# Linear attention on one core: the order of the last three heads, the engines that divide them, and the PSUM banks of the last numerators

## The chip, the cores and the metric

The kernel runs on one core of a Trainium2 chip. The metric is device time in microseconds for one execution. Three executions of the kernel before took 171.89 to 172.21 us, with a median of 172.04 us.

## The reference

Inputs q, k and v are bf16, each of shape (1, 32, 2048, 128): 32 heads, 2048 rows, 128 columns. For every head:

```
phi_q = where(q > 0, q + 1, exp(q)) + 1e-6
phi_k = where(k > 0, k + 1, exp(k)) + 1e-6
kv  = phi_k^T v          # 128 x 128
z   = sum of phi_k over the rows
num = phi_q kv           # 2048 x 128
den = phi_q z + 1e-6     # 2048
out = num / den
```

The kernel uses where(x > 0, x + 1, exp(x)) = min(exp(x), 1) + max(x, 0), and feeds the two summands to TensorE one after the other, so that PSUM adds them.

## The kernel before

**Tiles.** A head's 2048 rows lie as 128 partitions of 16 tiles ("tile" t, 0 to 15, each 128 columns wide). One head is 512 KB in each of k, v and q, and 512 KB of output. There are 6 input buffers per tensor (NBI) and 10 output buffers (NBO).

**Work of one head.**
- SP loads k, v and q (L255), one DMA each.
- ScalarE (ACT in the profile) takes exp of k (L263) and GpSimd (POOL) its positive part (L265). VectorE (DVE) makes min(exp, 1) + 1e-6 (L269, "emk"). For five of the 16 tiles, GpSimd adds the two parts (L274, the tag "phik").
- TensorE (PE) accumulates kv and z in one PSUM bank, kvz_ps (L285, L288). I call the block kv(h).
- ScalarE copies kv to kvs_sb (L294, "kvs"); VectorE adds z as its first column (L296, "zs").
- PE transposes q in two halves of 8 tiles into the two banks of xT_ps (L304). ScalarE takes exp of both halves (L315) and the positive part of the second half (L318, "relu"). VectorE takes the positive part of the first half (L321, "rq") and finishes emq (L324).
- PE multiplies phi_q with kvs (L333, L334) into the five banks of o_ps: three tiles to a bank, tile 15 split over banks 0 and 1. I call the block num(h).
- VectorE adds 1e-6 to the denominators (L352, "den"), inverts them (L356), and multiplies: tile 15 (L364), then tiles 0 to 5 and 6 to 14 (L369). For heads 30 and 31 the denominators are treated in two groups (banks 0 and 1, then 2 to 4), tiles 6 to 11 go to VectorE, and tiles 12 to 14 to ScalarE (L378, three instructions).
- SP stores the head (L394): one DMA, and three for head 31 (tiles 0 to 5, 6 to 11, 12 to 15).

**What sets the order.** Each piece of work is given to a small planner with an engine and a key (a number near the head's index). Each engine runs its pieces by rising key. The planner finds the dependences from named tags and puts in the semaphore waits. Two rules matter below: a piece that writes a bank waits for all readers of it on other engines, and two engines that read one bank take turns (L39). The list `place` (L239 to L242) sets keys by hand. The default keys of head h that matter are: on PE, kv h-1.2, transposes h-1.25, num h+0.7; on ScalarE, exp of q h-1.1, relu h-1.0, kvs h-0.95; on VectorE, zs h-0.095, rq h-1.052, emq h-1.045, den h+0.9. A store's key is h + 1.0 + 0.18 h, which puts the stores of the last heads behind all loads in SP's queue. The store waits for all the tiles that it holds, and SP issues in order. At the end SP waits for every output semaphore (L121).

In `place`, head 31 has its kv on PE at key 30.75, behind num(30), and its kvs and zs keys agree with that.

Of the kernel before, what the change touches and what calls it, by code (L numbers as in the profile page):

```python
# [4 lines left out]
ACT = mybir.ActivationFunctionType  # L5
ALU = mybir.AluOpType
P = 128
EPS = 1e-6
# [3 lines left out]
def _ap(base: bass.AP, elem_offset: int, dims):  # L12
    return bass.AP(base.tensor, base.offset + elem_offset, [list(base.ap[0])] + [list(d) for d in dims])
# [131 lines left out]
def bass_standalone__linear_attn_elu__prompt_kernel(  # L145
# [6 lines left out]
    B, H, S, D = q.shape  # L152
    assert D == P and S == 16 * P
    NT = 16
    NH = B * H
    bf16 = mybir.dt.bfloat16
    fp32 = mybir.dt.float32
    NBI = 6
    NBO = 10
    NC = D + 1  # L160
    NB = 5
# [4 lines left out]
    GAP, GRP = 32, 8 * D  # L166
    VW = 2 * GRP + 3 * GAP

    qf = q.rearrange("b h s d -> (b h) s d")
    kf = k.rearrange("b h s d -> (b h) s d")  # L170
    vf = v.rearrange("b h s d -> (b h) s d")
# [2 lines left out]
    with ExitStack() as es:  # L174
        def sb(name, shape, dt):
            return es.enter_context(nc.sbuf_tensor(name, shape, dt))
# [12 lines left out]
        rden_sb = sb("rden_sb", [P, 3, 4 * NB], fp32)  # L189
        o_sb = sb("o_sb", [P, NBO, NT, D], bf16)  # L190
        ident = sb("ident", [P, P], bf16)
        ones_sb = sb("ones_sb", [P, 1], bf16)

        xT_ps = es.enter_context(nc.psum_tensor("xT_ps", [P, NT * P], bf16))
        kvz_ps = es.enter_context(nc.psum_tensor("kvz_ps", [P, 512], fp32))
        o_ps = es.enter_context(nc.psum_tensor("o_ps", [P, NB * 512], fp32))

# [3 lines left out]
        def dma_sem(name):  # L201
            return dsems[name]

        for n, c in (("k", NBI), ("q", NBI), ("v", NBI), ("o", NBO + 2)):
            for i in range(c):
                dsems[(n, i)] = es.enter_context(nc.semaphore(f"s_{n}{i}"))

        block = es.enter_context(nc.Block())
        pl = Plan()

        def rows(x, h):
            return x[h].rearrange("(p j) d -> p (j d)", j=NT)

        ofull = o_ps[:, :]

        pl.add("pool", -9, lambda g: g.memset(ident[:], 0.0), writes=[("id0",)])
        pl.add("pool", -8, lambda g: g.affine_select(out=ident[:], in_=ident[:], compare_op=ALU.not_equal, fill=1.0,
# [1 line left out]
               reads=[("id0",)], writes=[("ident",)])  # L219
# [5 lines left out]
        def warm(n):  # L225

            def f(pe):
                for w in range(n):
# [10 lines left out]
        place = {("emk", 0): -2.05, ("rq", 0): -2.0, ("emq", 0): -1.9, ("zs", 0): -1.75,  # L239
                 ("emk", 1): -1.8, ("rq", 1): -1.7, ("emq", 1): -1.6, ("emk", 2): -1.4, ("rq", 2): 0.945,  # L240
                 ("ek", 1): -0.97, ("ek", 2): 0.03,
                 ("kv", NH - 1): NH - 2 + 0.75, ("kvs", NH - 1): NH - 2 + 0.05, ("zs", NH - 1): NH - 2 + 0.942}  # L242

        for h in range(NH):
            def at(name, key, h=h):
# [2 lines left out]
            bi, b2, b3, bo = h % NBI, h % 2, h % 3, h % NBO  # L248

            def load(name, buf, src, key, h=h, bi=bi):  # L250
                dst, rws = buf[:, bi], rows(src, h)
                if name == "v":
# [24 lines left out]

            def kv(pe, tiles, srcs, bi=bi, b3=b3):
                for j in tiles:
# [12 lines left out]
                   reads=[("emk", b3), ("rk", b3), ("v", bi), ("ones",), ("vones",)], writes=[("bankkv",)])  # L292
            pl.add("pe", at("kv", -1.2), lambda pe, kv=kv: kv(pe, ADD, (rk_sb,)), reads=[("phik", b3), ("v", bi)], writes=[("bankkv",)])
            pl.add("act", at("kvs", -0.95), lambda a, b3=b3: a.activation(kvs_sb[:, b3, 1:], kvz_ps[:, 1:NC], ACT.Copy),  # L294
                   reads=[("bankkv",)], writes=[("kvs", b3)])
            pl.add("dve", at("zs", -1 + 0.905), lambda d, b3=b3: d.tensor_scalar(  # L296
                kvs_sb[:, b3, 0:1], kvz_ps[:, 0:1], kvz_ps[:, NC:NC + 1], None, op0=ALU.add),
                   reads=[("bankkv",)], writes=[("zs", b3)])
# [14 lines left out]
            for half in (0, 1):  # L313
                pl.add("act", h - 1.1 + 0.05 * half,
                       lambda a, b2=b2, c=cols(half): a.activation(eq_sb[:, b2, c], xT_ps[:, c], ACT.Exp),  # L315
                       reads=[("bankx", half)], writes=[("eq", b2, half)])
            pl.add("act", h - 1.0,
                   lambda a, b3=b3, c=cols(1): a.activation(rq_sb[:, b3, c], xT_ps[:, c], ACT.Relu),  # L318
                   reads=[("bankx", 1)], writes=[("rq", b3, 1)])
            pl.add("dve", at("rq", -2 + 0.948),  # L320
                   lambda d, b3=b3, c=cols(0): d.tensor_scalar(rq_sb[:, b3, c], xT_ps[:, c], 0.0, None, op0=ALU.max),  # L321
                   reads=[("bankx", 0)], writes=[("rq", b3, 0)])
            pl.add("dve", at("emq", -2 + 0.955),
                   lambda d, b2=b2, b3=b3: d.tensor_scalar(emq_sb[:, b3, :], eq_sb[:, b2, :], 1.0, EPS, op0=ALU.min, op1=ALU.add),  # L324
                   reads=[("eq", b2, 0), ("eq", b2, 1)], writes=[("emq", b3)])


            phi = [("emq", b3), ("rq", b3, 0), ("rq", b3, 1), ("kvs", b3), ("zs", b3)]

            def num(bank, b3=b3):  # L330
                def tile(pe, t, col, c0, c1):
                    o_ap = o_ps[:, bank * 512 + col: bank * 512 + col + c1 - c0]
                    pe.matmul(o_ap, lhsT=emq_sb[:, b3, t * P:(t + 1) * P], rhs=kvs_sb[:, b3, c0:c1], start=True, stop=False)  # L333
                    return pe.matmul(o_ap, lhsT=rq_sb[:, b3, t * P:(t + 1) * P], rhs=kvs_sb[:, b3, c0:c1],  # L334
                                     start=False, stop=True)

                def f(pe):
                    for s in range(3):
                        last = tile(pe, bank * 3 + s, s * NC, 0, NC)
                    if bank < 2:  # L340
                        last = tile(pe, NT - 1, 3 * NC, 64 * bank, 64 * bank + 65)
                    return last
                return f
            for bank in range(NB):
                pl.add("pe", h + 0.7 + 0.001 * bank, num(bank), reads=phi, writes=[("banko", bank)])


            tail = h >= NH - 2
            for g, (b0, b1) in enumerate(((0, 2), (2, NB)) if tail else ((0, NB),)):
                key = h + 0.9 + 0.03 * g  # L350
                banks = [("banko", b) for b in range(b0, b1)]
                pl.add("dve", key, lambda d, b3=b3, b0=b0, b1=b1: d.tensor_scalar(  # L352
                    den_sb[:, b3, 4 * b0:4 * b1].rearrange("p (a b) -> p a b", b=4),
                    _ap(ofull, 512 * b0, [[512, b1 - b0], [NC, 4]]), EPS, None, op0=ALU.add),
                    reads=banks, writes=[("den", b3, g)])
                pl.add("dve", key + 0.01, lambda d, b3=b3, b0=b0, b1=b1: d.reciprocal(  # L356
                    rden_sb[:, b3, 4 * b0:4 * b1], den_sb[:, b3, 4 * b0:4 * b1]),
                    reads=[("den", b3, g)], writes=[("rden", b3, g)])

            def rd(col, dims, b3=b3):  # L360
                return _ap(rden_sb[:, b3, col:col + 1], 0, dims)

            def last_tile(d, bo=bo, rd=rd):
                return d.tensor_tensor(  # L364
                    out=o_sb[:, bo, NT - 1, :].rearrange("p (a b) -> p a b", b=64),
                    in0=_ap(ofull, 3 * NC + 1, [[512, 2], [1, 64]]), in1=rd(3, [[0, 2], [0, 64]]), op=ALU.mult)

            def div(b0, b1, bo=bo, rd=rd):
                return lambda d: d.tensor_tensor(  # L369
                    out=o_sb[:, bo, 3 * b0:3 * b1, :].rearrange("p (a b) d -> p a b d", b=3),  # L370
                    in0=_ap(ofull, 512 * b0 + 1, [[512, b1 - b0], [NC, 3], [1, D]]),
                    in1=rd(4 * b0, [[4, b1 - b0], [1, 3], [0, D]]), op=ALU.mult)

            def div_act(bank, bo=bo, rd=rd):
                def f(a):
                    for s in range(3):
                        c = 512 * bank + NC * s + 1
                        last = a.activation(o_sb[:, bo, 3 * bank + s, :], o_ps[:, c:c + D], ACT.Copy,  # L378
                                            scale=rd(4 * bank + s, [[1, 1]]))
                    return last  # L380
                return f

            lo, hi = ("rden", b3, 0), ("rden", b3, 1 if tail else 0)
            pl.add("dve", h + 0.92, last_tile, reads=[("banko", 0), ("banko", 1), lo], writes=[("o", bo, "t")])
            pl.add("dve", h + 0.925, div(0, 2), reads=[("banko", 0), ("banko", 1), lo], writes=[("o", bo, 0)])
            if tail:
                pl.add("dve", h + 0.945, div(2, 4), reads=[("banko", 2), ("banko", 3), hi], writes=[("o", bo, 1)])
                pl.add("act", h + 0.95, div_act(4), reads=[("banko", 4), hi], writes=[("o", bo, 2)])
            else:
                pl.add("dve", h + 0.945, div(2, NB), reads=[("banko", b) for b in (2, 3, 4)] + [hi],  # L390
                       writes=[("o", bo, 1), ("o", bo, 2)])

            def store(t0, t1, key, parts, slot, h=h, bo=bo):
                pl.add("sp", key, lambda sp: sp.dma_start(rows(of, h)[:, t0 * D:t1 * D],  # L394
                                                          o_sb[:, bo, t0:t1].rearrange("p j d -> p (j d)")),
                       reads=[("o", bo, p) for p in parts], dma=("o", slot))

            late = h + 1.0 + 0.18 * h
            if h < NH - 1:
                store(0, NT, late, ("t", 0, 1, 2), bo)  # L400
            else:
                store(0, 6, late, (0,), bo)
                store(6, 12, late + 0.01, (1,), NBO)
                store(12, 16, late + 0.02, ("t", 2), NBO + 1)

        pl.emit(block, sems, dma_sem)

# [27 lines left out]
```

## Time and profile before

| | |
|---|---|
| median of three executions | 172.04 us (171.89 to 172.21) |
| the profiled execution's own time | 171.87 us |
| its span, first to last instruction | 170.1 us |
| what lies around the span | 1.77 us |
| busy: PE, DVE, ACT, POOL | 158.0, 150.9, 155.0, 105.6 us |
| moved by DMA | 67.56 MB, mean 397 GB/s |
| mean granted TensorE clock | 0.99 |
| last VectorE multiplication ends | 166.43 us |
| last DMA lands | 169.6 us |

Times below are microseconds from the start of the span. "Landing" is the time from the issue of a DMA until the last of its 16 completion signals. The mean DMA share is that of 16 DMA engines, so 0.62 is about ten engines busy. In a list of instructions, a bracket shows how long the engine was idle just before and what released it.

### The profile page before, as it was taken

How to read it: one execution, taken by the hardware profiler on the slowest of the kernel's cores; microseconds unless marked ns; L12 is line 12 of the kernel's file. 1: busy time of each engine (PE TensorE's matmuls, PEld its weight loads, DVE VectorE, ACT ScalarE, POOL GpSimd, SP SyncE). 2: the span in 40 equal slices, each digit the busy share in tenths (PEclk: the TensorE clock that was granted, in tenths of full speed). 3: DMA queues.
4: the chain of work that ended last, by engine and by line, in shares of the span. 5: the costliest groups of instructions: out<-in, count | busy, mean ns of one | idle time of the engine just before them, and what ended most of it. 6: DMA issues, size and time to landing. Idle time of an engine off the chain costs nothing.

```text
span 170.1 us, 7091 instructions
## 1 busy us (share of the span) xinstructions
PE 158.0 (93%) x3108; PEld 155.8 (92%) x3108; DVE 150.9 (89%) x292; ACT 155.0 (91%) x167; POOL 105.6 (62%) x72
## 2 busy tenths in 40 slices
PE   6779999999999999999999999999999999997950
PEld 6669999999999999999999999999989999997940
DVE  0344999999999999999999999999998999999971
ACT  3899999999999999999999999999999999996331
POOL 3766777766666677766666667776666567655000
PEclk9999999999999999999999999999999999999996
DMA  5999999999999999999999999999999999999975
GB/s 220 333 415 408 418 408 406 415 412 408 411 411 412 411 417 411 412 414 410 412 416 410 413 414 410 409 416 413 411 416 412 413 412 411 412 415 413 410 302 196
DMA packets 22846, 67.56 MB, mean 397 GB/s; under 512 B 2080, under 2 KB 2464, under 8 KB 22816
## 3 DMA queue, kind: packets, MB, share of 16 engines
q1 hardware_dynamic: 22816, 67.12, 99.1%
q8 instruction: 24, 0.39, 0.9%
q14 instruction: 6, 0.05, 0.1%
HBM read 50.33 MB, written 16.78 MB: 395 GB/s over the span
## 4 chain that ended last, share of the span: by engine, by line
PE 68%; DVE 18%; DMA 6%; SPq 3%; issue 1%; ACT 0%; DVEq 0%
PE kvz_ps L285 29%; PE o_ps L333 13%; PE o_ps L334 13%; PE xT_ps L304 12%; DVE o_sb L369 8%; DMA v_sb<-in_v_dram 6%; SPq L255 3%; DVE rq_sb L321 2%; DVE emq_sb L324 2%; DVE emk_sb L269 2%; DVE o_sb L364 1%; DVE rden_sb L356 1%; PE kvz_ps L288 1%; DVE den_sb L352 1%; DVE kvs_sb L296 1%
## 5 line engine op out<-in xcount | busy, mean ns | idle before, releaser
L274 POOL TENSOR_TENSOR rk_sb<-rk_sb,emk_sb 128x640 bf16<-128x640 bf16 x32 | 44.7, 1398 | 46.9 <-DVE emq_sb L324 42.8
L369 DVE TENSOR_TENSOR o_sb<-o_ps,rden_sb 128x768 bf16<-128x768 f32 x64 | 70.1, 1134 | 0.0
L315 ACT ACTIVATE eq_sb<-xT_ps 128x1024 bf16<-128x1024 bf16 x64 | 66.7, 1170 | 3.1 <-PE xT_ps L304 3.0
L263 ACT ACTIVATE ek_sb<-k_sb 128x2048 bf16<-128x2048 bf16 x32 | 66.6, 2080 | 2.0 <-DMA k_sb<-in_k_dram 1.9
L285 PE MATMUL kvz_ps<-v_sb,rk_sb 128*128 128x128 bf16 (+1 forms) x512 | 67.0, 218 | 0.0
L333 PE MATMUL o_ps<-kvs_sb,emq_sb 128*128 128x129 bf16 (+1 forms) x544 | 62.0, 217 | 1.9 <-DVE o_sb L369 1.2
L265 POOL TENSOR_SCALAR rk_sb<-k_sb 128x2048 bf16<-128x2048 bf16 x32 | 60.7, 1896 | 3.8 <-DMA k_sb<-in_k_dram 3.0
L334 PE MATMUL o_ps<-kvs_sb,rq_sb 128*128 128x129 bf16 (+1 forms) x544 | 62.0, 217 | 0.0
L285 PE MATMUL kvz_ps<-v_sb,emk_sb 128*128 128x128 bf16 (+1 forms) x352 | 54.7, 218 | 2.6 <-DMA v_sb<-in_v_dram 1.1
L333 PEld LDWEIGHTS o_ps<-kvs_sb,emq_sb 128*128 128x128 bf16 x544 | 51.3, 98 | 2.3 <-DVE o_sb L369 1.5
L288 PE MATMUL kvz_ps<-ones_sb,rk_sb 128*128 128x1 bf16 x384 | 52.6, 165 | 0.0
L334 PEld LDWEIGHTS o_ps<-kvs_sb,rq_sb 128*128 128x128 bf16 x544 | 50.9, 97 | 0.0
L285 PEld LDWEIGHTS kvz_ps<-v_sb,rk_sb 128*128 128x128 bf16 x512 | 46.8, 97 | 0.0
L318 ACT ACTIVATE rq_sb<-xT_ps 128x1024 bf16<-128x1024 bf16 x32 | 37.8, 1180 | 0.0
L288 PE MATMUL kvz_ps<-ones_sb,emk_sb 128*128 128x1 bf16 x224 | 36.9, 166 | 0.0
L285 PEld LDWEIGHTS kvz_ps<-v_sb,emk_sb 128*128 128x128 bf16 x352 | 33.5, 97 | 3.6 <-DMA v_sb<-in_v_dram 2.4
L288 PEld LDWEIGHTS kvz_ps<-ones_sb,rk_sb 128*128 128x128 bf16 x384 | 35.0, 96 | 0.0
L304 PE MATMUL xT_ps<-ident,q_sb 128*128 128x128 bf16 x512 | 34.2, 220 | 0.5 <-DMA q_sb<-in_q_dram 0.4
L304 PEld LDWEIGHTS xT_ps<-ident,q_sb 128*128 128x128 bf16 x512 | 30.1, 98 | 1.1 <-DMA q_sb<-in_q_dram 0.9
L269 DVE TENSOR_SCALAR emk_sb<-ek_sb 128x2048 bf16<-128x2048 bf16 x32 | 21.8, 682 | 9.8 <-ACT ek_sb L263 9.8
L321 DVE TENSOR_SCALAR rq_sb<-xT_ps 128x1024 bf16<-128x1024 bf16 x32 | 21.7, 679 | 1.3 <-ACT eq_sb L315 1.3
L324 DVE TENSOR_SCALAR emq_sb<-eq_sb 128x2048 bf16<-128x2048 bf16 x32 | 22.0, 687 | 0.4 <-ACT eq_sb L315 0.4
(18 smaller groups left out, 79.2 us busy)
## 6 DMA issues: line engine op xcount, KB each, us to landing
k_sb<-in_k_dram SPq DMA_DIRECT2D x32, 512.0 KB, 13.6
q_sb<-in_q_dram SPq DMA_DIRECT2D x32, 512.0 KB, 13.1
v_sb<-in_v_dram SPq DMA_DIRECT2D x32, 512.0 KB, 13.4
out_dram<-o_sb SPq DMA_DIRECT2D x31, 512.0 KB, 13.7
out_dram<-o_sb SPq DMA_DIRECT2D x2, 192.0 KB, 3.2
out_dram<-o_sb SPq DMA_DIRECT2D x1, 128.0 KB, 2.8
```

The source lines that it names most:

```text
L263: lambda a, bi=bi, b2=b2: a.activation(ek_sb[:, b2, :], k_sb[:, bi, :], ACT.Exp),
L265: pl.add("pool", h, lambda g, bi=bi, b3=b3: g.tensor_scalar(rk_sb[:, b3, :], k_sb[:, bi, :], BIG, 0.0, op0=ALU.min, op1=ALU.max), reads=[( ...
L274: pl.add("pool", h + 0.5, lambda g, added=added: g.tensor_tensor(out=added(rk_sb), in0=added(rk_sb), in1=added(emk_sb), op=ALU.add), reads ...
L285: last = pe.matmul(kvz_ps[:, 1 - l:NC + r], lhsT=w, rhs=v_sb[:, bi, c - l:c + D + r], start=first, stop=fin, skip_group_check=True)
L288: last = pe.matmul(kvz_ps[:, 0:1], lhsT=w, rhs=ones_sb[:, 0:1], start=False, stop=fin, skip_group_check=True)
L304: last = pe.transpose(xT_ps[:, j * P:(j + 1) * P], q_sb[:, bi, j * P:(j + 1) * P], ident[:])
L315: lambda a, b2=b2, c=cols(half): a.activation(eq_sb[:, b2, c], xT_ps[:, c], ACT.Exp),
L318: lambda a, b3=b3, c=cols(1): a.activation(rq_sb[:, b3, c], xT_ps[:, c], ACT.Relu),
L324: lambda d, b2=b2, b3=b3: d.tensor_scalar(emq_sb[:, b3, :], eq_sb[:, b2, :], 1.0, EPS, op0=ALU.min, op1=ALU.add),
L333: pe.matmul(o_ap, lhsT=emq_sb[:, b3, t * P:(t + 1) * P], rhs=kvs_sb[:, b3, c0:c1], start=True, stop=False)
L334: return pe.matmul(o_ap, lhsT=rq_sb[:, b3, t * P:(t + 1) * P], rhs=kvs_sb[:, b3, c0:c1], start=False, stop=True)
L369: return lambda d: d.tensor_tensor(out=o_sb[:, bo, 3 * b0:3 * b1, :].rearrange("p (a b) d -> p a b d", b=3), in0=_ap(ofull, 512 * b0 + 1, ...
```

## The change

Only the pieces of heads 29, 30 and 31 change; the code for the others is rewritten so that it makes the same instructions in the same order.

- The two banks of transposed q become a float32 tensor x_ps of the same size, read as bf16 for the transposes. The numerators of head 31 for tiles 0 to 5 and 15 (banks 0 and 1) are written to it, not to o_ps.
- Head 29: VectorE divides tiles 0 to 5, 6 to 8 and 15; ScalarE divides tiles 9 to 14.
- Heads 30 and 31: VectorE divides tiles 0 to 2, 6 to 11 and 15; ScalarE divides tiles 3 to 5 and 12 to 14.
- kv(31) goes back to its default key 29.8 on PE, in front of num(30). On VectorE, rq(31) and emq(31) get keys in front of their default ones but behind the divisions of head 29; zs(31) stands right behind the first reciprocal of head 30. On ScalarE, kvs(31) stands behind the divisions of head 29 and in front of relu(31).
- Head 30 is stored in two DMAs (tiles 0 to 5, 6 to 15). Head 31 keeps three. One more output semaphore is there for this.

```diff
+    REST = ((0, NB, 0.9, (("dve", 0, 6), ("dve", 6, 15))),)
+    TAIL = {
+        NH - 3: ((0, NB, 0.9, (("dve", 0, 6), ("dve", 6, 9), ("act", 9, 15, 0.96))),),
+        NH - 2: ((0, 2, 0.9, (("dve", 0, 3), ("act", 3, 6, 0.96))),
+                 (2, NB, 0.93, (("dve", 6, 12), ("act", 12, 15, 0.97)))),
+        NH - 1: ((0, 2, 0.9, (("dve", 0, 3), ("act", 3, 6, 0.96))),
+                 (2, NB, 0.93, (("dve", 6, 12), ("act", 12, 15, 0.97)))),
+    }
+    PIECES = {NH - 2: ((0, 6), (6, NT)), NH - 1: ((0, 6), (6, 12), (12, NT))}
+    EXTRA = {NH - 2: 0, NH - 1: 1}
...
-        xT_ps = es.enter_context(nc.psum_tensor("xT_ps", [P, NT * P], bf16))
+        x_ps = es.enter_context(nc.psum_tensor("x_ps", [P, 1024], fp32))
...
-                 ("kv", NH - 1): NH - 2 + 0.75, ("kvs", NH - 1): NH - 2 + 0.05, ("zs", NH - 1): NH - 2 + 0.942}
+                 ("rq", NH - 1): NH - 3 + 0.925, ("emq", NH - 1): NH - 3 + 0.93, ("zs", NH - 1): NH - 2 + 0.9105,
+                 ("kvs", NH - 1): NH - 2 - 0.03}
...
+            def nbank(b, h=h):
+                return ("bankx", b) if h == NH - 1 and b < 2 else ("banko", b)
...
-                pl.add("pe", h + 0.7 + 0.001 * bank, num(bank), reads=phi, writes=[("banko", bank)])
+                pl.add("pe", h + 0.7 + 0.001 * bank, num(bank), reads=phi, writes=[nbank(bank)])
...
+            def div_act(t0, t1, bo=bo, rd=rd, nfull=nfull):
+                def f(a):
+                    for t in range(t0, t1):
+                        b, c = t // 3, 512 * (t // 3) + NC * (t % 3) + 1
+                        last = a.activation(o_sb[:, bo, t, :], _ap(nfull(b), c, [[1, D]]), ACT.Copy,
+                                            scale=rd(4 * b + t % 3, [[1, 1]]))
+                    return last
+                return f
...
+                for n, (eng, t0, t1, *place_a) in enumerate(runs):
+                    pl.add(eng, h + place_a[0] if eng == "act" else key + 0.012 + 0.004 * n,
+                           div_act(t0, t1) if eng == "act" else div(t0, t1),
+                           reads=[nbank(b) for b in range(t0 // 3, (t1 + 2) // 3)] + [("rden", b3, g)],
+                           writes=[("o", bo, t) for t in range(t0, t1)])
...
-            if h < NH - 1:
-                store(0, NT, late, ("t", 0, 1, 2), bo)
-            else:
-                store(0, 6, late, (0,), bo)
-                store(6, 12, late + 0.01, (1,), NBO)
-                store(12, 16, late + 0.02, ("t", 2), NBO + 1)
+            for n, (t0, t1) in enumerate(PIECES.get(h, ((0, NT),))):
+                store(t0, t1, late + 0.01 * n, bo if n == 0 else NBO + EXTRA[h] + n - 1)
```

More of the change, by code (lines that the diff above doesn't have):

```diff
@@ L202, in dma_sem @@
             return dsems[name]
-        for n, c in (("k", NBI), ("q", NBI), ("v", NBI), ("o", NBO + 2)):
+        for n, c in (("k", NBI), ("q", NBI), ("v", NBI), ("o", NBO + 3)):
             for i in range(c):
@@ L212, in rows @@
             return x[h].rearrange("(p j) d -> p (j d)", j=NT)
-        ofull = o_ps[:, :]
+        ofull, xfull = o_ps[:, :], x_ps[:, :]
+        xT_ps = xfull.bitcast(bf16)
         pl.add("pool", -9, lambda g: g.memset(ident[:], 0.0), writes=[("id0",)])
@@ L328, in bass_standalone__linear_attn_elu__prompt_kernel, with nfull, num @@
             phi = [("emq", b3), ("rq", b3, 0), ("rq", b3, 1), ("kvs", b3), ("zs", b3)]
-            def num(bank, b3=b3):
+            def nbank(b, h=h):
+                return ("bankx", b) if h == NH - 1 and b < 2 else ("banko", b)
+            def nfull(b, h=h):
+                return xfull if h == NH - 1 and b < 2 else ofull
+            def num(bank, b3=b3, nfull=nfull):
                 def tile(pe, t, col, c0, c1):
-                    o_ap = o_ps[:, bank * 512 + col: bank * 512 + col + c1 - c0]
+                    o_ap = _ap(nfull(bank), bank * 512 + col, [[1, c1 - c0]])
                     pe.matmul(o_ap, lhsT=emq_sb[:, b3, t * P:(t + 1) * P], rhs=kvs_sb[:, b3, c0:c1], start=True, stop=False)
@@ L344, in bass_standalone__linear_attn_elu__prompt_kernel @@
             for bank in range(NB):
-                pl.add("pe", h + 0.7 + 0.001 * bank, num(bank), reads=phi, writes=[("banko", bank)])
[L348 to L352, printed above, removed]
+                pl.add("pe", h + 0.7 + 0.001 * bank, num(bank), reads=phi, writes=[nbank(bank)])
@@ new lines, in bass_standalone__linear_attn_elu__prompt_kernel, with rd, last_tile, div @@
+            groups = TAIL.get(h, REST)
+            def rd(col, dims, b3=b3):
+                return _ap(rden_sb[:, b3, col:col + 1], 0, dims)
+            def last_tile(d, bo=bo, rd=rd, nfull=nfull):
+                return d.tensor_tensor(
+                    out=o_sb[:, bo, NT - 1, :].rearrange("p (a b) -> p a b", b=64),
+                    in0=_ap(nfull(0), 3 * NC + 1, [[512, 2], [1, 64]]), in1=rd(3, [[0, 2], [0, 64]]), op=ALU.mult)
+            def div(t0, t1, bo=bo, rd=rd, nfull=nfull):
+                b, nb, n = t0 // 3, max(1, (t1 - t0) // 3), min(3, t1 - t0)
+                return lambda d: d.tensor_tensor(
+                    out=o_sb[:, bo, t0:t1, :].rearrange("p (a b) d -> p a b d", b=n),
+                    in0=_ap(nfull(b), 512 * b + NC * (t0 % 3) + 1, [[512, nb], [NC, n], [1, D]]),
+                    in1=rd(4 * b + t0 % 3, [[4, nb], [1, n], [0, D]]), op=ALU.mult)
@@ new lines, in div_act @@
+            def div_act(t0, t1, bo=bo, rd=rd, nfull=nfull):
[6 more added lines that the diff above has]
+                return f
+            for g, (b0, b1, place_d, runs) in enumerate(groups):
+                key = h + place_d
+                banks = [nbank(b) for b in range(b0, b1)]
+                full = nfull(b0)
+                pl.add("dve", key, lambda d, b3=b3, b0=b0, b1=b1, full=full: d.tensor_scalar(
@@ L353, in bass_standalone__linear_attn_elu__prompt_kernel @@
                     den_sb[:, b3, 4 * b0:4 * b1].rearrange("p (a b) -> p a b", b=4),
-                    _ap(ofull, 512 * b0, [[512, b1 - b0], [NC, 4]]), EPS, None, op0=ALU.add),
+                    _ap(full, 512 * b0, [[512, b1 - b0], [NC, 4]]), EPS, None, op0=ALU.add),
                     reads=banks, writes=[("den", b3, g)])
@@ L358, in bass_standalone__linear_attn_elu__prompt_kernel @@
                     reads=[("den", b3, g)], writes=[("rden", b3, g)])
[L360 to L388, printed above, removed]
-            else:
-                pl.add("dve", h + 0.945, div(2, NB), reads=[("banko", b) for b in (2, 3, 4)] + [hi],
-                       writes=[("o", bo, 1), ("o", bo, 2)])
@@ L393, in store @@
-            def store(t0, t1, key, parts, slot, h=h, bo=bo):
+                if g == 0:
+                    pl.add("dve", h + 0.911, last_tile, reads=[nbank(0), nbank(1), ("rden", b3, 0)], writes=[("o", bo, NT - 1)])
+                for n, (eng, t0, t1, *place_a) in enumerate(runs):
[3 more added lines that the diff above has]
+                           writes=[("o", bo, t) for t in range(t0, t1)])
@@ L394, in store @@
+            def store(t0, t1, key, slot, h=h, bo=bo):
                 pl.add("sp", key, lambda sp: sp.dma_start(rows(of, h)[:, t0 * D:t1 * D],
                                                           o_sb[:, bo, t0:t1].rearrange("p j d -> p (j d)")),
-                       reads=[("o", bo, p) for p in parts], dma=("o", slot))
+                       reads=[("o", bo, t) for t in range(t0, t1)], dma=("o", slot))
             late = h + 1.0 + 0.18 * h
-            if h < NH - 1:
-                store(0, NT, late, ("t", 0, 1, 2), bo)
-            else:
-                store(0, 6, late, (0,), bo)
-                store(6, 12, late + 0.01, (1,), NBO)
-                store(12, 16, late + 0.02, ("t", 2), NBO + 1)
+            for n, (t0, t1) in enumerate(PIECES.get(h, ((0, NT),))):
+                store(t0, t1, late + 0.01 * n, bo if n == 0 else NBO + EXTRA[h] + n - 1)
```

## The prediction

> **What bounds the kernel now.** I began with the page: busy shares, chain of work, DMA queues.
>
> ```profile
> span 170.1 us, 7091 instructions
> PE 158.0 (93%) x3108; PEld 155.8 (92%) x3108; DVE 150.9 (89%) x292; ACT 155.0 (91%) x167; POOL 105.6 (62%) x72
> ...
> PE 68%; DVE 18%; DMA 6%; SPq 3%; issue 1%; ACT 0%; DVEq 0%
> ...
> q1 hardware_dynamic: 22816, 67.12, 99.1%
> q8 instruction: 24, 0.39, 0.9%
> ```
>
> Three engines are near 90%, and the chain lies mostly in PE and VectorE: compute seems to set the end. But data packets hold the 16 DMA engines for 99.1% of the span, so the end needs a second look. First the timeline of ScalarE near it:
>
> ```profile
> 161.82 0.28 ACT L294 ACTIVATE kvs_sb<-kvz_ps 128x128 bf16<-128x128 f32 x1 [2.93 <-PE kvz_ps L288]
> ```
>
> ScalarE waited 2.93 us for kv(31), which stood behind num(30) on PE; num(31) could begin only at 162.48. The change goes at this wait. Would an earlier last division end the kernel earlier? SP's timeline shows the issues of the stores of head 28, 29, 30, and of pieces one and three of head 31 (piece two: 166.45).
>
> ```profile
> 153.83 0.33 SPq L394 DMA_DIRECT2D out_dram<-o_sb  x1
> 158.56 0.33 SPq L394 DMA_DIRECT2D out_dram<-o_sb  x1
> 163.31 0.33 SPq L394 DMA_DIRECT2D out_dram<-o_sb  x1
> 165.12 0.33 SPq L394 DMA_DIRECT2D out_dram<-o_sb  x1
> 166.83 0.43 SPq L394 DMA_DIRECT2D out_dram<-o_sb  x1
> ```
>
> The DMA view, cut to windows round each of the six issues, has the us to landing in the last column:
>
> ```profile
> out_dram<-o_sb SPq DMA_DIRECT2D x1, 512.0 KB, 12.0
> out_dram<-o_sb SPq DMA_DIRECT2D x1, 512.0 KB, 8.5
> out_dram<-o_sb SPq DMA_DIRECT2D x1, 512.0 KB, 5.0
> out_dram<-o_sb SPq DMA_DIRECT2D x1, 192.0 KB, 3.6
> out_dram<-o_sb SPq DMA_DIRECT2D x1, 192.0 KB, 2.8
> out_dram<-o_sb SPq DMA_DIRECT2D x1, 128.0 KB, 2.8
> ```
>
> Issue plus landing: 165.83, 167.06, 168.31, 168.7, 169.25, 169.6. The landings of heads 28, 29 and 30 are 1.23 and 1.25 us apart, though their issues are 4.7 us apart; then 0.4 to 0.55 per 192 KB and 0.35 for 128 KB. These are steps of bytes, not of issues: on the DMA engines that land last, a queue never ran dry. The stretches by microsecond show the same (last two columns: DMA share, GB/s):
>
> ```profile
> 160.00:161.00 1.00, 1.00 (x27) 1.00 (x24) 0.97 (x3) 0.00 (x0) 0.00 (x0) 1.00 1.06 422
> 162.00:163.00 1.00, 0.52 (x10) 0.52 (x11) 0.80 (x2) 0.87 (x4) 0.00 (x0) 1.00 0.62 250
> 163.00:164.00 1.00, 1.00 (x22) 1.00 (x19) 0.71 (x4) 0.00 (x0) 0.00 (x0) 1.00 0.62 254
> 164.00:165.00 1.00, 0.55 (x10) 0.37 (x7) 1.00 (x2) 0.00 (x0) 0.00 (x0) 1.00 0.99 406
> ```
>
> From 162 to 164 the share is 0.62, ten engines of 16: six had run out of stores, ten were still behind. The trace also keeps the sixteen completion signals of each store. For head 28 the first is at 160.28 and the last at 165.79, so the engines are up to 5.5 us apart. By piece three of head 31, thirteen signal between 168.54 and 168.97; the last three, at 169.47 to 169.60, came 0.32 to 0.35 after their own signals for piece two, just the time of its bytes. **So three lagging DMA engines set the end, and compute does not.** The first signal of piece three came 1.71 after its issue; at that latency it could have been issued at 169.60 - 1.71 = 167.89, 1.06 us later than it was.
>
> **The change part by part.** The sum is made against the profiled execution (span 170.1, time 171.87). Heads 0 to 28 keep instructions and order, so they cost nothing new. The rest I ran through by hand.
>
> - *kv(31) in front of num(30).* PE ends the transposes of head 31 at 156.4. v of head 31 was issued at 141.71 and landed 12.8 later, at 154.5; phik(31) on GpSimd ends at 157.08 and only the last five tiles need it; zs(30), the last reader of the bank, ends at 155.90. So no wait: kv(31) runs its 2.16 us (159.62 to 161.78 before) from 156.4 to 158.5, in a gap that PE spent waiting for divisions (0.88 and 0.29 us). num(30) is queued behind it: 158.5, not 157.32.
> - *Six ScalarE tiles of head 29.* Three took 0.88, so six take 1.76. They stand behind exp of q, which ends at 157.97, and end at 159.65. VectorE's second division was 1.35 for nine tiles and becomes some 0.5. Banks 3 and 4 come free at 159.65 instead of 158.53, but num(30) gets to them only then: it ends at 160.45 (159.78 before, 0.7 later).
> - *kvs(31), then relu(31) on ScalarE.* kvs 159.65 to 159.9, relu (1.03) to 160.9. If kv(31) were late, kvs would hold up relu(31), and that num(31) in its new banks; but kv(31) is over by 158.5.
> - *VectorE, head 30.* rq and emq of head 31 end near 158.95. Denominators 159.5, reciprocal to 159.9, then zs(31), which waits for kvs(31) and has the divisions of head 30 queued behind it: 159.95 to 160.15. Tile 15, three tiles (0.5), second group, six tiles (0.95): to 162.2. ScalarE's six tiles end at 162.5.
> - *num(31).* Banks 0 and 1 now need only relu(31), 160.9, and are full at 161.85; banks 2 to 4 wait for head 30's divisions, 162.25, and take 1.2 (158.59 to 159.78): 163.45. Before, num(31) ran from 162.48 to 164.54.
> - *Head 31.* VectorE: first group from 162.2 to 163.4, second group 163.45 to 163.9, six tiles to 164.9. ScalarE ends beside it. Before, the last division ended at 166.43: **compute ends some 1.55 us earlier.**
> - *Stores.* Head 29 at 159.65 (1.1 later, with its lagging engines busy until 165.8 on head 28); head 30 at 161.65 and 162.5; head 31 at 163.5, 164.95, 165.3 (1.5 earlier). Each further issue holds SP some 0.4.
>
> On the lagging engines all this is hidden: they come to head 30 at 167.06 and to the last piece at 169.25, whenever those were issued. Earlier issues only lengthen their queue. What is late next, after the removed 2.93 us wait, is the DMA backlog, and it was late already.
>
> - *The added piece.* 32 KB per engine took 1.24, 12 KB 0.48, 8 KB 0.34. Bytes at (1.24 - 0.48)/20 KB = 0.038 us per KB leave 0.03 per DMA. So head 30 in two costs +0.03. From both sides: 0, as the bytes are the same; and 0.16, if the 12 KB take 0.55 (the longest such step) and the 20 KB go at the dearer price of the 8 KB row (0.34/8 x 20 = 0.85): 1.40 less 1.24. I take 0.04, nearest to the rows of 0.48.
> - *One more semaphore* for SP to wait on at the end: those waits took 28 ns each, and all but the last have passed before: 0.
>
> Sum: 170.1 + 0.04, a time of 171.9 for the profiled execution. That lies 0.17 below the median of the runs, 172.04; on the median it is 172.08. **Forecast: 172.1, no change.**
>
> **Rivals.**
>
> *A: the gain of compute goes through.* For it: the page's chain ends in PE and VectorE. Against: the steps between landings. If the backlog were gone in timed runs, all 1.55 would count: 172.04 - 1.55 = 170.5. The Trainium skill, "DMA: Bandwidth & Descriptors" (Anatomy of one DMA), has a rule for this, fitted on DMAs issued by GpSimd: a DMA takes some 2.0 us plus its bytes at 436 GB/s, so an end that moves with the last issue. By it 128 KB would land 2.3 us after its issue (estimate); the row has 2.8, and 5.0 for head 30 where the rule gives 3.2. Chance 0.12.
>
> *B: one more instruction fetch on a lagging engine.* On the page, queue q8 made 24 fetches of 0.39 MB in all, 16 KB each, at 0.9% of 16 engines' span: 0.009 x 16 x 170.1 / 24 = 1.02 us of one DMA engine each. ScalarE gets 12 more instructions. If these, or moved waits, bring one more fetch to one of the last three engines before 169, the end moves by 1.02: 173.1. Against: TensorE, with the longest program, gets no more matrix products, and 12 instructions are few beside 7091. Chance 0.08. The Trainium skill, "Runtime: NRT & Kernel Launch" (Instruction fetch mechanics), also has 16 KiB blocks and calls their cost mostly hidden; here each takes an engine from the stores for 1.02 us.
>
> *C: the change does not do what it says.* kv(31) or kvs(31) could wait after all, and compute end where it did. As the last issue has 1.06 us to spare even now, the time is the same, 172.1. Chance 0.05.
>
> **How the numbers follow.** Forecast 0.75, C 0.05, A 0.12, B 0.08. A measurement of this kernel can tell about 0.2%, 0.34 us: faster 0.12, same 0.75 + 0.05 = 0.80, slower 0.08. The range: below, the fourth-slowest engine signals 0.5 to 0.6 before the last three, so a new deal of fetches could bring 0.5: 171.5. Above, 0.16 for the piece and the 0.17 by which runs go over their median, 172.4, and 0.1 for a part of B: 172.5. A and B lie outside, 0.20 together.
>
> **What would show it.** Right: the last division near 164.9, the last issue near 165.3, and still a last landing near 169.6, piece three landing over 4 us after its issue, with no idle wait of ScalarE before kvs(31). The steps for heads 28 and 29 stay 1.2. Wrong: if the last landing follows the last issue by 2.8 and the span shrinks by over 0.5 (A), or q8 shows 25 fetches and the steps a jump of 1 us (B).

## The result, and the profile after

The changed kernel took 172.32 us (median of 20 executions, 171.53 to 172.48), the kernel before, measured beside it, 171.94 us (median of 20, 171.03 to 172.29). The ratio is 1.0022, with a 95% interval of 1.0012 to 1.0031. Measured once more as a control (below), the same program gave 1.0008, interval 0.9993 to 1.0024. So the change brought no gain, and at most 0.2 to 0.3% of loss. The profiled execution took 172.26 us.

The page of the changed kernel, rows that answer to those of before (span, busy time, chain by engine, DMA queues):

```profile
span 170.3 us, 7108 instructions
PE 158.0 (93%) x3108; PEld 156.5 (92%) x3108; DVE 149.2 (88%) x292; ACT 157.8 (93%) x179; POOL 105.6 (62%) x72
...
PE 86%; DMA 4%; DVE 3%; ACT 3%; issue 1%; SPq 0%
...
q1 hardware_dynamic: 22960, 67.12, 99.0%
q8 instruction: 24, 0.39, 0.9%
```

Compute did what the change asks of it. The timeline of ScalarE shows six divisions of head 29 (1.67 us), then kvs(31) at 159.57, with no idle time in front of it where there were 2.93 us:

```profile
158.07 1.67 ACT L392 ACTIVATE o_sb<-o_ps,rden_sb 128x128 bf16<-128x128 f32 x6
159.57 0.33 ACT L311 ACTIVATE kvs_sb<-kvz_ps 128x128 bf16<-128x128 f32 x1
159.73 1.09 ACT L335 ACTIVATE rq_sb<-x_ps 128x1024 bf16<-128x1024 bf16 x1
```

VectorE's timeline ends with the last multiplication, at 163.92 + 0.96 = 164.88, where the kernel before ended at 166.43:

```profile
163.92 0.96 DVE L383 TENSOR_TENSOR o_sb<-o_ps,rden_sb 128x768 bf16<-128x768 f32 x1
```

So compute ends 1.55 us earlier, and the span is 0.2 us longer. SP's timeline and the DMA view (in windows round each issue) show where the 1.55 us went. The issues, for head 29, for the two pieces of head 30, and for the three of head 31 (the last row holds two, the second at 165.29):

```profile
159.81 0.33 SPq L417 DMA_DIRECT2D out_dram<-o_sb  x1
161.66 0.33 SPq L417 DMA_DIRECT2D out_dram<-o_sb  x1
162.44 0.33 SPq L417 DMA_DIRECT2D out_dram<-o_sb  x1
163.78 0.33 SPq L417 DMA_DIRECT2D out_dram<-o_sb  x1
164.91 0.81 SPq L417 DMA_DIRECT2D out_dram<-o_sb  x2
```

Their sizes and us to landing, in the same order:

```profile
out_dram<-o_sb SPq DMA_DIRECT2D x1, 512.0 KB, 7.4
out_dram<-o_sb SPq DMA_DIRECT2D x1, 192.0 KB, 6.1
out_dram<-o_sb SPq DMA_DIRECT2D x1, 320.0 KB, 6.1
out_dram<-o_sb SPq DMA_DIRECT2D x1, 192.0 KB, 5.2
out_dram<-o_sb SPq DMA_DIRECT2D x1, 192.0 KB, 4.6
out_dram<-o_sb SPq DMA_DIRECT2D x1, 128.0 KB, 4.6
```

The last 128 KB waited 4.6 us from issue to landing instead of 2.8: the 1.5 us by which they were issued earlier became time in a queue. Issue plus landing gives 167.2, 167.8, 168.5, 169.0, 169.5, 169.9, steps of 0.5 per 192 KB, 0.8 for 320 KB and 0.35 for 128 KB. A step follows the bytes of a store, not the time of its issue.

The stretches by microsecond (last two columns: DMA share, GB/s) show the engines running out one after another; in the last of these rows the share is 0.60, about ten engines of 16. By the completion signals, seven engines had finished their part of the last piece by 167.14, and the other nine signalled it between 168.46 and 169.86:

```profile
165.00:166.00 1.00, 0.00 (x0) 0.00 (x0) 0.00 (x0) 0.00 (x0) 0.00 (x0) 0.57 0.77 304
166.00:167.00 1.00, 0.00 (x0) 0.00 (x0) 0.00 (x0) 0.00 (x0) 0.00 (x0) 0.50 0.86 325
167.00:168.00 1.00, 0.00 (x0) 0.00 (x0) 0.00 (x0) 0.00 (x0) 0.00 (x0) 0.50 0.60 227
```

For nearly five microseconds, from 164.88 to 169.86, no compute engine does anything, and the DMA engines are the only thing left.

### The profile page after: what moved, and what is told of

Its sections match the earlier page's. It is cut to its first block, busy times and chain, and to the rows that moved or that the text cites. A ratio compares the mean times of both kernels' runs of the same rounds, so it can differ in the third digit from the quotient of the medians.

```text
span 170.3 us, 7108 instructions
## 1 busy us (share of the span) xinstructions
PE 158.0 (93%) x3108; PEld 156.5 (92%) x3108; DVE 149.2 (88%) x292; ACT 157.8 (93%) x179; POOL 105.6 (62%) x72
## 3 DMA queue, kind: packets, MB, share of 16 engines
q1 hardware_dynamic: 22960, 67.12, 99.0%
## 4 chain that ended last, share of the span: by engine, by line
PE 86%; DMA 4%; DVE 3%; ACT 3%; issue 1%; SPq 0%
PE kvz_ps L302 36%; PE o_ps L356 17%; PE o_ps L357 16%; PE x_ps L321 15%; DMA v_sb<-in_v_dram 4%; DVE o_sb L383 1%; ACT eq_sb L332 1%; PE kvz_ps L305 1%; ACT ek_sb L280 1%; ACT rq_sb L335 1%; DVE rden_sb L405 1%; SPq L272 0%; DVE emk_sb L286 0%; DVE den_sb L401 0%; DVE o_sb L377 0%
## 5 line engine op out<-in xcount | busy, mean ns | idle before, releaser
L332 ACT ACTIVATE eq_sb<-x_ps 128x1024 bf16<-128x1024 bf16 x64 | 70.8, 1300 | 3.0 <-PE x_ps L321 3.0
L280 ACT ACTIVATE ek_sb<-k_sb 128x2048 bf16<-128x2048 bf16 x32 | 70.5, 2204 | 1.9 <-DMA k_sb<-in_k_dram 1.9
L302 PE MATMUL kvz_ps<-v_sb,rk_sb 128*128 128x128 bf16 (+1 forms) x512 | 68.4, 220 | 0.0
L383 DVE TENSOR_TENSOR o_sb<-o_ps,rden_sb 128x768 bf16<-128x768 f32 (+2 forms) x63 | 68.0, 1119 | 0.1
L356 PE MATMUL o_ps<-kvs_sb,emq_sb 128*128 128x129 bf16 (+1 forms) x536 | 61.1, 217 | 0.3 <-DVE o_sb L383 0.3
L302 PE MATMUL kvz_ps<-v_sb,emk_sb 128*128 128x128 bf16 (+1 forms) x352 | 55.8, 220 | 2.5 <-DMA v_sb<-in_v_dram 1.1
L335 ACT ACTIVATE rq_sb<-x_ps 128x1024 bf16<-128x1024 bf16 x32 | 42.0, 1313 | 0.0
L321 PE MATMUL x_ps<-ident,q_sb 128*128 128x128 bf16 x512 | 33.8, 219 | 0.8 <-DMA q_sb<-in_q_dram 0.7
L321 PEld LDWEIGHTS x_ps<-ident,q_sb 128*128 128x128 bf16 x512 | 29.9, 98 | 1.1 <-DMA q_sb<-in_q_dram 1.1
L338 DVE TENSOR_SCALAR rq_sb<-x_ps 128x1024 bf16<-128x1024 bf16 x32 | 21.8, 680 | 2.0 <-ACT eq_sb L332 2.0
```

The costliest lines, as they stand in the source:

```text
L280: lambda a, bi=bi, b2=b2: a.activation(ek_sb[:, b2, :], k_sb[:, bi, :], ACT.Exp),
L302: last = pe.matmul(kvz_ps[:, 1 - l:NC + r], lhsT=w, rhs=v_sb[:, bi, c - l:c + D + r], start=first, stop=fin, skip_group_check=True)
L321: last = pe.transpose(xT_ps[:, j * P:(j + 1) * P], q_sb[:, bi, j * P:(j + 1) * P], ident[:])
L383: return lambda d: d.tensor_tensor(out=o_sb[:, bo, t0:t1, :].rearrange("p (a b) d -> p a b d", b=n), in0=_ap(nfull(b), 512 * b + NC * (t0 ...
```

## The experiments

Two theories were tested. **Backlog**: the DMA engines that lag set the end, and compute does not. **Rival**: the end follows the last divisions, and in the changed kernel the smaller pieces ate what compute gained.

### Three stores left out, in both kernels

```diff
-            for n, (t0, t1) in enumerate(PIECES.get(h, ((0, NT),))):
+            for n, (t0, t1) in enumerate(() if h in (21, 23, 25) else PIECES.get(h, ((0, NT),))):
```

The edit of the kernel before is the same in its own code.

> The kernel before without the stores of heads 21, 23 and 25 (those heads of the output are left unwritten); nothing else is changed. Backlog theory (three lagging DMA engines set the end): they have 3 x 1.24 = 3.7 us less to do, but the last piece is still issued near 166.83, and an engine without a queue signals it 1.71 us later, at 168.55; the end comes 1.05 us earlier, 171.94 - 1.05 = 170.9. Rival (the end follows the last divisions; in the changed kernel the smaller pieces ate what compute gained): compute is not touched, so 171.9.

> The changed kernel without the stores of heads 21, 23 and 25 (left unwritten). Backlog theory: the lagging engines would end 3.7 us earlier, at 166.1; the last issue at 165.27 plus 1.71 gives 167.0, so the end comes 2.9 us earlier: 172.32 - 2.9 = 169.4, and 1.5 us under the kernel before with the same stores left out, which is what compute gained. Rival (pieces ate the gain): 172.3, not faster than the other.

Measured: the kernel before took 170.51 us with three stores less (ratio to the whole kernel 0.9926, interval 0.9906 to 0.9945), the changed one 169.69 (0.9870, 0.9845 to 0.9895). In the first, the stretch from 163 to 164 shows DMA engines with nothing to do (share 0.07):

```profile
163.00:164.00 1.00, 1.00 (x21) 1.00 (x19) 0.71 (x5) 0.00 (x0) 0.00 (x0) 1.00 0.07 29
```

SP's timeline of that kernel (two issues, the second at 166.64) and the landing of the last piece:

```profile
166.27 0.81 SPq L394 DMA_DIRECT2D out_dram<-o_sb  x2
```

```profile
out_dram<-o_sb SPq DMA_DIRECT2D x1, 128.0 KB, 2.0
```

The same two views of the changed kernel without the three stores (second issue at 165.41):

```profile
165.03 0.81 SPq L417 DMA_DIRECT2D out_dram<-o_sb  x2
```

```profile
out_dram<-o_sb SPq DMA_DIRECT2D x1, 128.0 KB, 2.0
```

Without a backlog the last landing follows the last issue by 2.00 us in both: 168.64 and 167.41. Now the changed kernel is the faster one, by 0.8 us in the medians and 1.2 us in the profiled spans (169.1 and 167.9); the last issues of these two executions are 1.23 apart. Of the 1.5 expected, the medians show about half and the spans most; each profiled execution was the slowest of its series. The medians were expected at 170.9 and 169.4 and came at 170.51 and 169.69; why the kernel before gained 0.4 more is not shown. Compute itself hardly moved in the profiled executions: the last issues were at 166.83 and 165.29 with all stores. The rival, which expected no effect of the stores, falls.

### The last divisions made later

```diff
+        scratch = sb("scratch", [P, 2, HALF], bf16)
...
-                   lambda a, b3=b3, c=cols(1): a.activation(rq_sb[:, b3, c], xT_ps[:, c], ACT.Relu),
+                   lambda a, b3=b3, c=cols(1), n=(2 if h == NH - 1 else 0): [
+                       a.activation(scratch[:, i, :], xT_ps[:, c], ACT.Relu) for i in range(n)] and None or
+                       a.activation(rq_sb[:, b3, c], xT_ps[:, c], ACT.Relu),
```

The second kernel has 4 for 2.

> The changed kernel with two more copies of the relu of head 31 on ScalarE, into a scratch tile, ahead of the real one: the numerators of head 31, and all behind them, come 2 x 1.03 = 2.06 us later. Backlog theory: the last piece is issued near 167.3, still 0.8 us ahead of what the lagging engines need (169.53 - 1.38 = 168.15), so the time stays 172.3. Rival (end follows the last divisions): 172.3 + 2.1 = 174.4.

> The same with four copies: 4.1 us later. Backlog theory: 2.9 us of it are covered, the last piece is issued near 169.4 and ends 1.7 us later at 171.1; 172.3 + 1.25 = 173.6. Rival: 172.3 + 4.1 = 176.4.

Measured, two copies: 171.91 us, ratio 1.0009 (0.9993 to 1.0024). The last issue came at 166.40 in the profile, 1.1 us later than in the changed kernel and not 2.1: the real relu began only 1.5 later (161.21, where it had been 159.73), and the wait of TensorE for the divisions of head 30 ahead of the last banks (0.3 us in the changed kernel) went. The time did not move. The DMA view has the landing of the last piece:

```profile
out_dram<-o_sb SPq DMA_DIRECT2D x1, 128.0 KB, 3.1
```

It took 3.1 us, where it had been 4.6: the delay was taken out of the queue. Four copies: 173.94 us, ratio 1.0111 (1.0078 to 1.0143). The last issue came at 170.04, 4.75 later than in the changed kernel and not 4.1. The real relu began 3.5 later, and num(31) behind it took longer: TensorE had been idle for 3.97 us ahead of it, and its granted clock was 0.50 while num(31) ran, where the changed kernel has 1.00. The landing of the last piece shows an empty queue:

```profile
out_dram<-o_sb SPq DMA_DIRECT2D x1, 128.0 KB, 2.1
```

The backlog covered 4.75 us but for the last part: the last landing moved from 169.86 to 172.10, by 2.24. So 2.5 us of lateness in compute were free in the changed kernel, where the expectation had 2.9.

### The control, and the pieces alone

```diff
-    PIECES = {NH - 2: ((0, 6), (6, NT)), NH - 1: ((0, 6), (6, 12), (12, NT))}
-    EXTRA = {NH - 2: 0, NH - 1: 1}
+    PIECES = {NH - 1: ((0, 6), (6, 12), (12, NT))}
+    EXTRA = {NH - 1: 0}
```

This is the changed kernel with head 30 whole. The kernel before with head 30 cut:

```diff
-            if h < NH - 1:
+            if h < NH - 2:
                 store(0, NT, late, ("t", 0, 1, 2), bo)
+            elif h == NH - 2:
+                store(0, 6, late, (0,), bo)
+                store(6, NT, late + 0.01, ("t", 1, 2), NBO + 2)
```

> The changed kernel once more, as the control for the three below. Its first measurement was 0.38 us over the kernel before. Backlog theory: 0.05 of that is the added piece of head 30, and the rest is how far behind the slowest DMA engine fell in the first 15 us, before any changed instruction, so it is scatter between executions: ratio 1.000 to 1.001 here. Rival (something in the changed program costs 0.4 us in every execution): 1.002 again.

> The changed kernel with head 30 stored in one DMA. Backlog theory: the lagging engines spend 1.24 on it and not 0.49 + 0.79, so 0.04 less than the control. Rival (smaller pieces ate what compute gained): 0.4 us or more less than the control.

> The kernel before with head 30 stored in two DMAs (tiles 0 to 5, 6 to 15), that part of the change alone. Backlog theory: +0.04 us, ratio 1.000. Rival (pieces are dear): 1.002.

Measured: control 171.80 us, 1.0008 (0.9993 to 1.0024); head 30 whole 171.95 us, 1.0008 (0.9996 to 1.0020); kernel before with head 30 cut 171.81 us, 1.0001 (0.9985 to 1.0017). The pieces cost nothing that can be measured, which ends the rival's second half. In the landings, the two pieces take 0.49 + 0.79 = 1.28 us on the slowest engine, against 1.24 for the whole.

### kv(31) back behind the numerators of head 30

```diff
-                 ("rq", NH - 1): NH - 3 + 0.925, ("emq", NH - 1): NH - 3 + 0.93, ("zs", NH - 1): NH - 2 + 0.9105,
-                 ("kvs", NH - 1): NH - 2 - 0.03}
+                 ("rq", NH - 1): NH - 3 + 0.925, ("emq", NH - 1): NH - 3 + 0.93, ("zs", NH - 1): NH - 2 + 0.9425,
+                 ("kv", NH - 1): NH - 2 + 0.75, ("kvs", NH - 1): NH - 2 + 0.05}
```

> The changed kernel with kv(31) back behind the numerators of head 30, and its kvs and zs with it; all other parts stay. Compute gives back most of its 1.5 us, the last issue is near 166.5 instead of 165.3. Backlog theory: the time stays within 0.1 of the control. Rival (end follows the last divisions): 1.2 us over the control.

Measured: 172.13 us, ratio 1.0010 (0.9996 to 1.0024). The timeline of ScalarE has the wait for kv(31) again:

```profile
161.96 0.28 ACT L311 ACTIVATE kvs_sb<-kvz_ps 128x128 bf16<-128x128 f32 x1 [2.03 <-PE kvz_ps L305]
```

The last issue came at 166.59, 1.3 us later than in the changed kernel. The median is 0.33 us over the control's, more than the 0.1 expected, but the ratios (1.0010 and 1.0008) and their intervals do not tell them apart; 1.2 us are excluded.

### Where the lag comes from: fewer instructions

```diff
-                        if not l + r:
-                            last = pe.matmul(kvz_ps[:, 0:1], lhsT=w, rhs=ones_sb[:, 0:1], start=False, stop=fin,
-                                             skip_group_check=True)
...
-                    pe.matmul(o_ap, lhsT=emq_sb[:, b3, t * P:(t + 1) * P], rhs=kvs_sb[:, b3, c0:c1], start=True, stop=False)
-                    return pe.matmul(o_ap, lhsT=rq_sb[:, b3, t * P:(t + 1) * P], rhs=kvs_sb[:, b3, c0:c1],
-                                     start=False, stop=True)
+                    return pe.matmul(o_ap, lhsT=emq_sb[:, b3, t * P:(t + 1) * P], rhs=kvs_sb[:, b3, c0:c1], start=True, stop=True)
```

> Where the lag of the three DMA engines comes from. The changed kernel without the one-column products (L305, 608) and without the second half of each numerator (L357, 544): z and the numerators are incomplete. Each product is two instructions, so TensorE's program is 2304 instructions shorter, and at 24 fetches for 6216 there are some 9 fetches fewer. Theory (each fetch takes about 1.0 to 1.4 us of one DMA engine, and the three that lag have had three of the 24): the slowest have two, the last landing comes 1.0 to 1.4 us earlier, 172.0 - 1.2 = 170.8. Rival (these engines are slower in themselves, or are held up by the loads): nothing but compute changes, which does not set the end: 172.0.

The kernel leaves out the one-column products and the second half of each numerator. Measured: 170.50 us, ratio 0.9918 (0.9896 to 0.9940), 1.35 us under the kernel before, measured beside it (171.85). Span, fetch queue and last piece on its page:

```profile
span 168.7 us, 4804 instructions
...
q8 instruction: 15, 0.25, 0.5%
...
out_dram<-o_sb SPq DMA_DIRECT2D x1, 128.0 KB, 7.0
```

Nine fetches fewer, and for head 28 the completion signals spread over 3.75 us (160.69 to 164.44), where the changed kernel has 5.76 (160.24 to 166.00). The data that the stores and loads move are the same, 67.12 MB. That speaks for the fetches. But TensorE also worked less in this kernel, and compute ran ahead: the last piece was issued at 161.24, 4.05 earlier than in the changed kernel. It landed only 1.61 earlier, at 168.25, so here too the issue does not set the end. The first engine signals head 28 no earlier (160.69, against 160.24); it is the last one that gained.

The completion signals of the kernel before show more directly what a fetch does. From one DMA to the next, all sixteen signals move on by nearly the same 1.2 to 1.3 us, until a fetch. Here are two loads of k in a row, issued at 4.04 and 5.04, each as us behind its first signal; a fetch of 16 KB ran from 12.80 to 13.85:

```
issued   signals, us behind the first
4.04     0.00 0.13 0.16 0.20 0.24 0.31 0.32 0.33 0.38 0.54 0.66 0.87 1.03 1.23 1.32 1.33
5.04     0.00 0.13 0.17 0.21 0.25 0.31 0.33 0.34 0.57 0.65 0.86 1.01 1.21 1.29 1.31 2.07
```

One engine went from 0.38 to 2.07, and the other fifteen kept their places. The kernel before has 24 fetches and, from 11 us to head 28, 24 such jumps: one engine falls back by 1.3 to 2.3 us (mean 1.6), and its signal comes 2.0 to 3.0 us after a fetch began. Otherwise no engine fell back by more than 0.9. In the kernel with fewer instructions, 14 of the 15 fetches have such a jump (1.5 to 1.7 us). So it is the fetches that make the engines drift apart, beyond the 1.3 us that they are apart at 11 us already. The slowest engine signalled head 28 1.56 us earlier in the kernel with fewer instructions, which fits one jump fewer.

### Which engines lag, and an attempt to relieve them

```diff
+            if h == 23:
+                for n, (p0, p1) in enumerate(zip(CUT, CUT[1:])):
+                    store(0, NT, late + 0.01 * n, NBO + 3 + n, p0=p0, p1=p1)
```

Here `store` takes a range of partitions. The first of two such kernels cut three stores at 8, 88 and 104; in the second CUT is 0, 1, 3, 6, 10, 15, 21, 28, 128.

> Which DMA engines lag. The changed kernel with three stores cut by partitions, each in two DMAs: head 21 at 8, head 23 at 88, head 25 at 104. A DMA over 8, 40, 88, 104, 24 or 120 partitions may not use all 16 engines, and its completion signals then show the lag of those it uses. Theory (the lag sits in fixed engines): some of these DMAs end well before the others. The time is 172 to 174, as the engines that are used get more. Rival (every DMA is spread over all 16): all of them end with the same spread of 5.5 us as their neighbours, and the time is 172.2.

> Which of the first eight DMA engines lag. The changed kernel with the store of head 23 cut by partitions into DMAs of 1, 2, 3, 4, 5, 6, 7 and 100 partitions; in the run before, 8 partitions had 8 completion signals, three of them 3.2 us or more behind the other five. If a DMA of n partitions uses the first n engines, each further size adds the signal of one more engine. Theory (the engines that fetch instructions are neighbours, and the three that lag most are the first of them): sizes 1 to 5 end early, and 6 and 7 have a signal 3 us later. Rival (no such order): a late signal already in one of the sizes 1 to 5. The time is of no use here: the 100 partitions go over ten engines, which costs the lagging ones 0.3 us and more, 172.5 to 173.5.

Measured, once each: 174.01 and 172.60 us. Apart from one signal within 1.9 us of its issue, a store over n partitions had n completion signals for n from 1 to 8, ten for 40 and 100, eleven for 88, twelve for 24, thirteen for 104, fifteen for 120. So a cut store uses part of the engines. In the first kernel the store over 8 partitions ended at 155.87, ahead of the rest of its head at 157.03; the signals of the five other cut stores spread over 5.4 to 6.4 us. That decides little between theory and rival. In the second kernel the signals of the small stores were:

```
partitions   signals (us)
1            153.96
2            154.14 154.34
3            154.32 154.48 154.52
4            154.51 154.67 154.71 156.69
5            154.69 154.87 154.89 156.89 157.64
6            154.88 155.05 155.08 157.07 157.82 157.85
7            155.07 155.24 155.26 157.27 158.00 158.03 158.05
```

Each size shows the signals of the one above it about 0.2 later, and one more. The first three engines do not lag, the fourth is 2 us behind them, and the next three are about 3 us behind. So through these seven stores the lag stays with the same engines, and these are neighbours, as the theory had it. But a late signal came already at size 4, which was the rival's sign and not the theory's. In the first of these kernels, three of the eight signals of the store over 8 partitions were late, not four: so which engines are late is not quite the same in every kernel.

That points to a kernel that should beat both: give bytes to the three engines that do not lag.

```diff
+    SHIFT = {24: ((0, NT, 0, 51), (0, NT, 51, 64), (0, NT, 64, P)),
+             26: ((0, 8, 0, 51), (0, 8, 51, 64), (0, 8, 64, P), (8, NT, 0, P))}
```

> Bytes moved off the lagging DMA engines, compute untouched. In the changed kernel the stores of head 24, and of half the tiles of head 26, are cut at partitions 51 and 64: by the run before, 51 = 3 x 17 partitions go over engines 0 to 2, which do not lag, 17 on each; 13 go over 13 engines, 64 over all. Engines 0 to 2 get 22 partitions for 8, the lagging ones 5 for 8. Backlog theory: a partition of 4 KB takes 0.155 us, so a lagging engine has 3 x 0.155 x 1.5 = 0.70 less and three more DMAs at 0.037, 0.59 less in all; engines 0 to 2 (1.1 behind the first) come to 4.5 and stay under the rest. 172.0 - 0.6 = 171.4 at unchanged compute, and below both kernels. Rival (another engine, or the number of DMAs, sets the end): 172.0 or more.

Measured: 171.88 us against 172.06, ratio 0.9988 (0.9970 to 1.0007). The direction is the expected one, but the interval takes in 1, and 0.6 us were not reached. In the completion signals the slowest engine went from head 22 (158.57) to head 28 (165.61) in 7.04 us, where the changed kernel took 7.46 and the kernel before 7.50: some 0.45 us of relief in the profiled executions, of 0.59 expected. It is not shown that this kernel is faster.

## Why the prediction was right

Its forecast was no change, 172.1 us, by a DMA backlog that hides 1.55 us of compute. Point by point:

- **The bound.** Shown by three kinds of run: with three stores less the changed kernel took 2.2 us less than the whole kernel before (171.79 x 0.013) and was the faster of the two; a last issue 1.1 us later cost nothing; one 4.75 us later cost 2.24. Another rival, that all engines together were held up by the memory, does not fit the landings of the kernel before: on the slowest engine a store of 512 KB took 1.25 us (head 23) and 1.26 (head 24) with all engines at work, and 1.24 (head 26) with about ten (share 0.62).
- **Compute.** The last multiplication was forecast for 164.9 and ended at 164.88; the last issue for 165.3 and came at 165.29; head 29 for 159.65 and came at 159.81; head 30 for 161.65 and 162.5 and came at 161.66 and 162.44. ScalarE's idle time before kvs(31) went. Rival C, a change that does not do what it says, is out.
- **The last landing.** Forecast 169.64, measured 169.86. The added piece cost 0.04 to 0.05 as taken. The other 0.21 was there before any changed instruction: the slowest engine signals head 28 at 166.00 and not 165.79, and it signals the third load of k at 13.15 and not 12.94. From head 29 to the end it took 2.61 and 2.56 us. In the control's profiled execution the last landing was at 169.67. How near the time came to the forecast is partly luck: two series of the same program had medians of 172.32 and 171.80.
- **The slack of the last issue**, put at 1.06 us, was too large. The term that failed is the latency without a queue: I took 1.71 from the first engine's signal, but the last engine's signal counts, 2.00 to 2.06 in the kernels without a backlog. So the slack in that execution was 169.60 - 2.00 - 166.83 = 0.77. It moved neither the forecast nor the range.
- **Rival A**, the gain goes through: out, by the same runs. The rule that the Trainium skill gives for DMAs issued by GpSimd ("DMA: Bandwidth & Descriptors", Anatomy of one DMA: some 2.0 us plus bytes) comes near where there is no queue, 2.0 measured for 128 KB against the 2.3 estimated from it; it says nothing of 4.6 us in a queue.
- **Rival B**, one more fetch: did not happen, 24 fetches on both pages. Its price was too small. The 1.02 us is the time of a fetch's packet; an engine fell back by 1.6 in the mean, so one more fetch on the slowest engine would have given some 172.04 + 1.6 = 173.6 (an estimate) and not 173.1. Nine fetches fewer went with 1.35 us, near the price of one jump.
- **What stays open.** The first series lies 0.22% over the kernel before, just past the bound that I set for no change. The two series of the changed kernel gave 1.0022 and 1.0008, its variants with two copies, with head 30 whole and with the late kv(31) 1.0009, 1.0008 and 1.0010. All intervals but the first take in 1. A loss of some 0.1% may be there; the piece of head 30 is not its cause, since the kernel with head 30 whole gave the same 1.0008 as the control. Nothing run here settles it.

## What to carry to other kernels

When a store's landing times step by bytes while its issues lie further apart, a queue sets the end, and earlier issues only wait longer; look at this before shortening the compute that comes last. The chain of waits does not show it, since it follows instructions, and the average DMA share hides it, because some engines are empty while others are behind. What can help then is less work on the engines that are behind: three stores less took 1.3 to 2.2 us off, and nine fetches less went with 1.35.

## What the runs showed of the hardware

- The sixteen DMA engines drift apart during the run. In the kernel before, the signals of one DMA spread over 0.5 us at the first load and 5.5 us at head 28. The page of the Trainium skill on this ("Runtime: NRT & Kernel Launch", Instruction fetch mechanics) calls the cost of crossing a 16 KiB block mostly hidden. It was not hidden here: the 24 fetches took 0.97 us each, and each set one DMA engine back by 1.3 to 2.3 us; with 15 of them the kernel was 1.35 us faster, though it also had fewer matrix products.
- A 128 KB store into an empty queue had its last signal 2.00 us (twice) and 2.06 us after its issue; a further DMA on a busy engine cost only some 0.04 us (1.28 for head 30 in two, 1.24 whole).
- A store over 51 = 3 x 17 partitions had three completion signals, one over 13 had thirteen, one over 100 ten: the number of partitions decides how many engines a store uses.
- In the kernel with four copies TensorE was idle for 3.97 us before the last numerators and ran them at a granted clock of 0.50. With two copies it was idle for 2.15 us, and the clock was 1.00.
